# A loop over key places for the PV products of a decode-attention kernel, with fewer small products and one buffer for most of wo

## The chip, the cores and the metric

One core of a Trainium2 chip. The time is device microseconds (us) of one execution. The kernel before takes 357.53 us, the median of 3 runs (356.9 to 357.56).

Ratios are the mean time of one kernel's fast runs over that of the kernel before's fast runs of the same rounds, with a 95% interval, so they are not quite the quotient of the medians that are quoted beside them. The traces are of one profiled run each.

## The reference

One decode step of a transformer block with conditioned layer norms (cut to what matters; q has 32 heads, the caches 8 kv heads, so 4 q heads share a kv head; 32768 key places of 128 elements, all bfloat16):

```python
mod = silu(c) @ w_mod                       # six vectors: sa, ca, ga, sb, cb, gb
h = layernorm(x) * (1 + ca) + sa
q = (h @ wq)                                # 32 heads x 128
scores = q . k_cache * 128 ** -0.5          # per kv head: 4 x 32768
p = softmax(scores)
o = p @ v_cache                             # "PV"
x = x + ga * (o @ wo)
h = layernorm(x) * (1 + cb) + sb
x = x + gb * (relu(h @ w1) @ w2)
```

The K and V caches are 64 MiB each; with the weights the core reads 149 MB in one step.

## The kernel before

All big reads go through one DMA queue in a fixed order into a ring of four buffers. A buffer holds half of one kv head's K or V (4 MB); V of a head comes interleaved with K of the next head.

```python
ring = ctx.enter_context(tc.tile_pool(name="ring", bufs=4))
stream = [("wm",), ("wq",)] + [("k", 0, (2 * G, 2 * G + 1)) for G in range(NG)]
for g in range(LAST):
    for G in range(NG):
        stream += [(kind, gg, (2 * G, 2 * G + 1)) for kind, gg in (("k", g + 1), ("v", g))]
```

For each half of K, `scores` transposes it on VectorE in four pieces (`KTt`, three buffers) and multiplies on TensorE (`S_ps`, 32 products). `softmax` has three steps. The first takes the maximum (`m_p`, `mT_ps`, `Mrow`, `Mexp`). The second sends it back to all partitions (`Mb_ps` on TensorE, `nbias`), takes the exponential on ScalarE (`P_g`) and transposes it on VectorE (`PT_g`). The third is the sum and its reciprocal (`L_ps`, `Linv`). `pv` multiplies the transposed probabilities with V: 16 products for each 2 MB of V, so 32 for a buffer.

```python
def pe_order(instr):
    tc.stamp_issue_order_token(instr.ins, "pe_pv")    # keeps TensorE's order as written
# ... in pv:
    for j in js:
        m = nc.tensor.matmul(
            o_tiles[g][:], lhsT=PT_g[:, j, REP * s0:REP * (s0 + 4)],
            rhs=Vsb.rearrange("p (s j) d -> p s j d", j=16)[:, :, j, :],
            start=(u == 0 and j == 0), stop=(u == end and j == 15),
        )
        pe_order(m)
# ... in the main loop, for the second half of a head's V:
    stages = softmax(g + 1)
    pv(g, 2 * G, range(8))
    next(stages)                       # step 2 of the next head's softmax
    pv(g, 2 * G, range(8, 16))
    next(stages)
    pv(g, 2 * G + 1)
    next(stages, None)
```

So the author had put the steps of the next head's softmax between PV products, with order tokens that hold the scheduler to it.

## Time and profile before

| What | Number | Read from |
|---|---|---|
| span of the profiled run | 356.0 us | page, first line |
| queue of the big reads | 98.0% of the span | page, queues |
| a 4 MB tile, landing to landing | 9.67 us | landings in the trace |
| four tiles (a head) | 38.7 us | 4 x 9.67 |
| second PV of head 0 begins | 83.82 us | timeline |
| second PV of head 6 begins | 315.15 us | timeline |
| from there to the end of the span | 40.9 us | 356.0 - 315.15 |

The two starts give the **head period** used in this whole document: (315.15 - 83.82) / 6 = 38.56 us, the stream's pace. For every kernel below the span is cut the same way: start of the second PV of head 0, six heads, and the rest.

Two lines of the DMA queue's own waits (waited for: total us, times, longest) show what frees the buffers:

```profile
SPq L118 <- DVE KTt L375: 134.3, 15, 12.4
SPq L118 <- PE o_ps L458: 72.3, 8, 9.9
```

The queue waits for VectorE and TensorE to give buffers back, but the packets in flight keep the DMA engines busy all the while: the DMA row has a nine in 38 of its 40 slices, and the queue fills 98.0% of the span. So these waits cost nothing here.

### The profile page before, as it was taken

How to read it: one execution, taken by the hardware profiler on the slowest of the kernel's cores; microseconds unless marked ns; L12 is line 12 of the kernel's file. 1: busy time of each engine (PE TensorE's matmuls, PEld its weight loads, DVE VectorE, ACT ScalarE, POOL GpSimd, SP SyncE). 2: the span in 40 equal slices, each digit the busy share in tenths (PEclk: the TensorE clock that was granted, in tenths of full speed). 3: DMA queues.
4: the chain of work that ended last, by engine and by line, in shares of the span. 5: the costliest groups of instructions: out<-in, count | busy, mean ns of one | idle time of the engine just before them, and what ended most of it. 6: DMA issues, size and time to landing. Idle time of an engine off the chain costs nothing.

```text
span 356.0 us, 3635 instructions
## 1 busy us (share of the span) xinstructions
PE 287.1 (81%) x1571; PEld 128.5 (36%) x1571; DVE 191.6 (54%) x219; ACT 34.0 (10%) x78; POOL 8.5 (2%) x14
## 2 busy tenths in 40 slices
PE   0466965999699969788896969896978879799874
PEld 0253322444334433334332334333333424244473
DVE  8524697782667366463819373746637290842020
ACT  1023003102100110012000200012000200011020
POOL 9000000000000000000000000000000000000000
PEclk9966789999879998999899969999899969899755
DMA  8999999999999999999999999999999999999993
GB/s 326 437 435 436 423 443 427 422 446 427 429 438 435 420 447 431 423 442 429 431 438 427 433 439 423 438 436 423 435 442 419 442 431 422 442 427 419 390 407 138
DMA packets 6602, 149.66 MB, mean 420 GB/s; under 512 B 697, under 2 KB 698, under 8 KB 1594
## 3 DMA queue, kind: packets, MB, share of 16 engines
q1 hardware_dynamic: 6578, 149.43, 98.0%
q8 instruction: 12, 0.20, 0.2%
q14 instruction: 4, 0.03, 0.0%
q10 hardware_dynamic: 8, 0.00, 0.0%
HBM read 149.42 MB, written 0.00 MB: 420 GB/s over the span
## 4 chain that ended last, share of the span: by engine, by line
DMA 55%; PE 22%; DVE 16%; issue 4%; ACT 1%; SPq 0%; DVEq 0%; ACTq 0%
DMA Ksb<-in_A_k_cache_dram 50%; DVE KTt L375 14%; PE S_ps L384 9%; PE o_ps L458 6%; DMA c_row<-in_c_dram 3%; DMA w_sb<-in_B_w_dram 2%; PE modT_ps L284 1%; PE acc_ps L448 1%; PE q_ps L267 1%; PE mod_ps L267 1%; PE a_ps L510 1%; PE qT_ps L334 1%; PE acc_ps L468 1%; PE acc_ps L530 1%; ACT L243 0%
## 5 line engine op out<-in xcount | busy, mean ns | idle before, releaser
L384 PE MATMUL S_ps<-KTt,qbd 128*128 128x512 bf16 x512 | 135.6, 423 | 39.1 <-DVE KTt L375 39.1
L375 DVE STREAM_TRANSPOSE KTt<-Ksb 128x2048 f32<-128x2048 f32 x64 | 142.5, 2280 | 34.4 <-DMA Ksb<-in_A_k_cache_dram 32.8
L458 PE MATMUL o_ps<-Vsb,PT_g 128*16 128x512 bf16 x480 | 108.4, 379 | 0.0
L384 PEld LDWEIGHTS <-qbd 128*128 128x128 bf16 x512 | 53.4, 105 | 114.8 <-issue 64.4
L458 PEld LDWEIGHTS <-PT_g 128*16 128x16 bf16 x480 | 40.8, 90 | 60.0 <-issue 6.0
L390 DVE TENSOR_SCALAR_CACHE_REDUCE S_g<-S_ps 128x512 f32<-128x512 f32 x16 | 11.1, 692 | 37.7 <-PE S_ps L384 37.7
L355 ACT COPY qbd<-qrep_sb 32x128 bf16<-32x128 bf16 x32 | 9.4, 295 | 161.5 <-PE S_ps L384 160.4
L427 DVE STREAM_TRANSPOSE PT_g<-P_g 128x1024 bf16<-128x1024 bf16 x8 | 9.9, 1238 | 21.7 <-ACT P_g L422 21.7
L482 DVE TENSOR_TENSOR oT_sb<-acc_ps,Linv 128x4 bf16<-128x4 f32 x8 | 1.3, 162 | 25.7 <-PE acc_ps L448 17.2
L468 PE MATMUL acc_ps<-osel,X 16*128 16x4 f32 x64 | 8.4, 250 | 3.2 <-ACT X L466 3.2
L419 ACT ACTIVATE nbias<-Mb_ps 128x1 f32<-128x1 f32 x8 | 1.4, 171 | 89.1 <-PE Mb_ps L417 89.1
L203 PE MATMUL xc_ps<-one,c_bd 8*128 8x1 bf16 x4 | 0.3, 171 | 11.8 <-DVE c_bd L193 11.8
L468 PEld LDWEIGHTS acc_ps<-osel,X 16*128 16x128 f32 x64 | 7.7, 186 | 4.3 <-ACT X L466 4.3
L422 ACT ACTIVATE P_g<-S_g,nbias 128x1024 bf16<-128x1024 f32 x8 | 9.2, 1149 | 0.4 <-ACT nbias L419 0.2
L155 DVE COPY sel<-ident_bf 128x128 bf16<-128x128 bf16 x4 | 7.2, 3544 | 0.0
L466 ACT COPY X<-o_ps 16x512 f32<-16x512 f32 x8 | 4.6, 574 | 22.8 <-PE o_ps L458 22.8
L406 DVE TENSOR_REDUCE Mrow<-mT_ps 1x4 f32<-1x128 f32 x8 | 2.2, 278 | 8.2 <-PE mT_ps L404 8.2
L267 PE MATMUL q_ps<-wq_sb,hT 128*1 128x512 bf16 x32 | 3.6, 627 | 2.6 <-DVE hT L250 2.6
L435 DVE RECIPROCAL Linv<-L_ps 128x4 f32<-128x4 f32 x8 | 1.4, 176 | 7.0 <-PE L_ps L433 7.0
L417 PEld LDWEIGHTS Mb_ps<-ident_f,Mexp 1*128 1x128 f32 x16 | 2.3, 182 | 6.1 <-issue 6.1
L203 PEld LDWEIGHTS <-c_bd 8*128 8x128 bf16 x4 | 0.2, 112 | 11.8 <-DVE c_bd L193 11.8
L284 PE MATMUL modT_ps<-rowsel,mod_rows 128*128 128x4 f32 x16 | 3.9, 375 | 0.5 <-ACT mod_rows L279 0.5
(112 smaller groups left out, 96.6 us busy)
## 6 DMA issues: line engine op xcount, KB each, us to landing
Ksb<-in_A_k_cache_dram SPq DMA_DIRECT2D x16, 4096.0 KB, 29.7
Vsb<-in_A_v_cache_dram SPq DMA_DIRECT2D x15, 4096.0 KB, 28.9
wq_sb<-in_A_wq_dram SPq DMA_DIRECT2D x1, 4096.0 KB, 18.8
Vsb<-in_A_v_cache_dram SPq DMA_DIRECT2D x2, 2048.0 KB, 16.3
wm_sb<-in_w_mod_dram SPq DMA_DIRECT2D x1, 3072.0 KB, 10.3
wo_sb<-in_A_wo_dram SPq DMA_DIRECT2D x1, 2048.0 KB
wo_sb<-in_A_wo_dram SPq DMA_DIRECT2D x2, 1024.0 KB, 9.9
w_sb<-in_B_w_dram SPq DMA_DIRECT2D x1, 1792.0 KB, 9.9
```

Of the source, the lines that this page charges most:

```text
L155: nc.vector.tensor_copy(out=sel[:, hp, :].rearrange("p (a c) -> p a c", a=4), in_=src)
L267: nc.tensor.matmul(dst[j // 4][32 * (j % 4):32 * (j % 4) + 1, :], lhsT=src_T[:, kt:kt + 1], rhs=w[:, kt, j * 512:(j + 1) * 512], start=(kt ...
L284: nc.tensor.matmul(modT_ps[:, i, ko, :], lhsT=mod_rows[:, i, :].rearrange("q (m ko) -> q ko m", ko=KT)[:, ko, :], rhs=rowsel[:], start=Tru ...
L355: nc.scalar.copy(out=o, in_=i)
L375: nc.vector.transpose(out=KTt[:].bitcast(F32), in_=Ksb[:, 32 * half:32 * half + 32, :].rearrange("p j d -> p (j d)").bitcast(F32),)
L384: nc.tensor.matmul(S_ps, lhsT=qbd[g % 2][:, hp, s, :], rhs=KTv[:, 16 * sl:16 * sl + 16, h, :, par], start=(t4 == 0 and sl == 0 and hp == 0 ...
L390: nc.vector.tensor_scalar(out=S_tiles[g][:, G, :], in0=S_ps, scalar1=1.0, scalar2=None, op0=ALU.mult, op1=ALU.max, accum_out=m_tiles[g][:, ...
L422: nc.scalar.activation(out=P_g[:], in_=S_g[:].rearrange("p g f -> p (g f)"), func=ACT.Exp, bias=nbias[:], scale=scale, accum_out=l_g[:],)
L427: nc.vector.transpose(out=PT_g[:], in_=P_g[:])
L458: m = nc.tensor.matmul(o_tiles[g][:], lhsT=PT_g[:, j, REP * s0:REP * (s0 + 4)], rhs=Vsb.rearrange("p (s j) d -> p s j d", j=16)[:, :, j, : ...
L466: nc.scalar.copy(out=X[:], in_=o_tiles.pop(g)[:])
L468: nc.tensor.matmul(oT_ps, lhsT=X[:, s * Dh:(s + 1) * Dh], rhs=osel[:, s, :], start=(s == 0), stop=(g < LAST and s == 3), skip_group_check= ...
```

## The change

Its intent: write PV once as a loop that TensorE itself runs, to have fewer copies of instructions and less instruction fetch; replace many small TensorE products in the head and tail by a few larger ones; and put wo of the first six kv heads into one buffer of the ring, so that a slot is spared near the end. The core of the diff (cut):

```diff
-    WOP = [(0, Hkv // 2), (Hkv // 2, Hkv // 4), (3 * Hkv // 4, Hkv // 4)]
+    WOP = [(0, Hkv // 4), (Hkv // 4, Hkv // 2), (3 * Hkv // 4, Hkv // 4)]
...
-    stream += [("v", LAST, (0, 1)), ("v", LAST, (2,)), ("wo", 0), ("wo", 1), ("v", LAST, (3,)), ("wo", 2)]
+    stream += [("v", LAST, (0, 1)), ("v", LAST, (2,)), ("wo_mid", 0, 1), ("v", LAST, (3,)), ("wo", 2)]
...
-    def pe_order(instr):
-        tc.stamp_issue_order_token(instr.ins, "pe_pv")
...
+            nc.vector.memset(o_tiles[g][:], 0.0)
+        NJ = 4 // len(us)
+        PTv = PT_g.rearrange("p (a b) c -> p a b c", b=NJ)
+        with tc.tile_critical():
+            with nc.tensor.Fori(0, 16 // NJ) as turn:
+                for b in range(NJ):
+                    for u, V in zip(us, Vs):
+                        c0 = REP * 4 * (u % 2)
+                        nc.tensor.matmul(
+                            o_tiles[g][:], lhsT=PTv[:, bass.DynSlice(turn, 1), b, c0:c0 + 4 * REP],
+                            rhs=V.rearrange("p (s a b) d -> p s a b d", s=4, b=NJ)[:, :, bass.DynSlice(turn, 1), b, :],
+                            start=False, stop=False, skip_group_check=True,
+                        )
...
-            nc.scalar.copy(out=X[:], in_=o_tiles.pop(g)[:])
-            for s in range(4):
-                nc.tensor.matmul(oT_ps, lhsT=X[:, s * Dh:(s + 1) * Dh], rhs=osel[:, s, :], ...)
+        nc.vector.tensor_tensor(out=X[:], in0=o_tiles.pop(g)[:]..., in1=smask[:]..., op=ALU.mult)
+        nc.vector.tensor_reduce(out=Y[:], in_=X[:].rearrange("p s d -> p d s"), op=ALU.add, axis=AX.X)
+        nc.tensor.matmul(oT_ps, lhsT=Y[:], rhs=qsel, ...)
...
-                stages = softmax(g + 1)
-                pv(g, 2 * G, range(8))
-                next(stages)
-                pv(g, 2 * G, range(8, 16))
-                next(stages)
-                pv(g, 2 * G + 1)
-                next(stages, None)
+            if g < LAST or G == 0:
+                pv(g, (2 * G, 2 * G + 1))
                 continue
+        if g + 1 < Hkv:
+            stages = softmax(g + 1)
+            next(stages)
```

A loop makes 8 turns of 4 products for a 4 MB tile of V. It stands in a critical section, that is, in a block of its own. Since the loop is one piece, softmax's steps can no longer stand between its products, and the order tokens went with them.

## The prediction

> **What bounds the kernel now.** I read the page first (busy shares, the DMA row, the groups, the issues), then the wait list of the DMA queue, then the timeline of one head and of the tail. Page:

> ```profile
> span 356.0 us, 3635 instructions
> ...
> DMA  8999999999999999999999999999999999999993
> ...
> q1 hardware_dynamic: 6578, 149.43, 98.0%
> q8 instruction: 12, 0.20, 0.2%
> ...
> L384 PE MATMUL S_ps<-KTt,qbd 128*128 128x512 bf16 x512 | 135.6, 423 | 39.1 <-DVE KTt L375 39.1
> L375 DVE STREAM_TRANSPOSE KTt<-Ksb 128x2048 f32<-128x2048 f32 x64 | 142.5, 2280 | 34.4 <-DMA Ksb<-in_A_k_cache_dram 32.8
> L458 PE MATMUL o_ps<-Vsb,PT_g 128*16 128x512 bf16 x480 | 108.4, 379 | 0.0
> ...
> Ksb<-in_A_k_cache_dram SPq DMA_DIRECT2D x16, 4096.0 KB, 29.7
> Vsb<-in_A_v_cache_dram SPq DMA_DIRECT2D x15, 4096.0 KB, 28.9
> ```

> The stream is the bound: one queue fills 98.0% of the span. A 4 MB tile takes 29 us from issue to landing but tiles land about 9.67 us apart (landings at 283.25 and 292.92 us), so about three of the four slots are always in flight and compute has slack. A head is four tiles, 38.7 us. The timeline shows how that slack is made:

> ```profile
> 239.95 3.62 PE L458 MATMUL o_ps<-Vsb,PT_g 128*16 128x512 bf16 x16
> ...
> 240.26 1.15 ACT L422 ACTIVATE P_g<-S_g,nbias 128x1024 bf16<-128x1024 f32 x1
> ...
> 241.53 1.25 DVE L427 STREAM_TRANSPOSE PT_g<-P_g 128x1024 bf16<-128x1024 bf16 x1 [3.08 <-ACT P_g L422]
> ...
> 245.66 8.88 DVE L375 STREAM_TRANSPOSE KTt<-Ksb 128x2048 f32<-128x2048 f32 x4
> 248.02 8.78 PE L384 MATMUL S_ps<-KTt,qbd 128*128 128x512 bf16 x32 [2.73 <-DVE KTt L375]
> ...
> 256.72 7.07 PE L458 MATMUL o_ps<-Vsb,PT_g 128*16 128x512 bf16 x32
> ```

> The next head's softmax (exponential, transposition) runs on the other engines while TensorE does PV. Then one half-head is transpositions, 32 score products, 32 PV products. PV costs 7.07/32 = 0.221 us a product.

> The tail (the chain of waits, near its end):

> ```profile
> 331.74 0.58 ACT X L466
> ...
> 335.19 2.69 PE a_ps L510 x24
> ...
> 343.24 1.21 PE acc_ps L518 x32
> ...
> 344.46 7.63 DMA w_sb<-in_B_w_dram
> ```

> The last weight piece lands at 352.10, the span ends 3.9 us later; the tail on TensorE is only just ahead of the last bytes.

> [...] L448 issues 64 weight loads and products in 1.84 us, 29 ns a pair. [...] after the 2.73 us gap before 248.02 the 32 score products take 8.78 us, against 7.07 for 32 PV products. [...]

> **The change part by part.**

> Removed: copies of PV instructions (480 static products become 16 loops, 496 products), 64 small products of V tile 2 of the last head, three of every four products with osel, many small products in the head, some instruction fetch. Fetch is 0.2% of the DMA time; in the head and middle all this lies beside the stream. Value at most 1 us.

> Added, and decisive: each loop stands in a critical section, hence in its own block. The built program's TensorE list shows three things.
> a) Before every loop TensorE waits for the semaphores of *all* earlier work in program order, including the K tile issued after the V tile it needs. The loop of V(g,0) waits for K(g+1,1), one landing (9.67 us) later than before. About two tiles would still be in flight, so this alone does not drain the queue.
> b) Nothing crosses a block's edge. The softmax of head g+1 begins (max) before the second loop of head g, but its second step (Mb, exponential, transposition, sum) comes only after that loop. On VectorE it stands ahead of the next four K transpositions. So softmax and scores, once beside PV, follow it in series.
> c) Per product in the loop: one register instruction of several fused steps, then a product with two register addresses; per turn of four, an add and a compare-and-branch.

> Cost of a product, c[...] c = 0.272 us, above the 0.221 of the static product, so the sequencer sets the pace. A loop of 32: 8.7 us, plus about 0.6 for waits, drain and branches (my estimate): 9.3 us.

> After a first loop (half B): K has landed and three of four transpositions ran during the loop. 32 products 7.1, then the maxima 0.69+0.08+0.15, the transposition 0.3, Mrow 0.28, gaps 0.2: 8.8 us.

> After a second loop (half A): mask X about 0.7 (as the 0.69 of the scores' copy), Mexp 0.2, Mb and nbias about 0.55, exponential 1.15, transposition 1.25, Lexp 0.2, sum and reciprocal 0.7: 4.8. Then 11.1 from the first K transposition to the last score (245.66 to 256.80 in the timeline, half clock included), then the copy 0.8: 16.7 us.

> A head: 2 x 9.3 + 8.8 + 16.7 = 44.1 us against 38.7 of the stream. The bound moves from the DMA to this serial cycle of TensorE and VectorE.

> Path: the second loop of head 0 waits for K(2,0), which lands at 89.4 (99.08 - 9.67). Six heads on, 89.4 + 6 x 44.1 = 354.0, the second loop of head 6 begins. It ends at 363.3; softmax of head 7, now bare, 4.9: 368.2; its first loop 9.3: 377.5; the loop of V tile 2, 16 products: 5.0: 382.5; X, Y and a product 1.6; wo's rows 2.7; copy and join 2.7; 64 small products 1.8: 391.3. From there as before without its DMA wait: to w1's products 4.7, these 1.7, relu 0.2, w2's 1.8: 399.7. End of span 3.4 later: 403.1. Times stand about 1.5 above the span (357.53 against 356.0): **405 us**, 13% slower. Of the 47 us, some 33 come from six heads of 5.4 us; most of the rest from the tail, whose 7.1 us PV loops now wait for softmax and weights are asked for later.

> wo in one buffer: it frees a slot, so V tile 3 waits for the loop of V(6,1) rather than of V(7,0,1), one loop earlier; hidden behind the late TensorE chain. Worth 0 to 1 us.

> **The rivals.**
> R1, the stream stays the bound: c stays at or under 0.22. Then a head is 2 x 7.7 + 25.5 = 40.9 us, still over 38.7, and the path ends about 464 products x 0.051 = 24 us earlier: about 381. For it: the array itself can do 0.221. Against it: even then the series in (b) exceeds the stream.
> R2, all is hidden: the barrier's waits are met and softmax overlaps in some way I misread; the stream still ends near 350 and the time is 355 to 359. For it: DMA at 98% and 29 us of flight, deep slack. Against it: program order on TensorE puts Mb after the loop, and no slack in buffers cures a serial cycle longer than the stream's.
> R3, register addressing is dear, c = 0.35 to 0.40 us (fused steps taken one by one): 464 x 0.08 to 0.13 = 36 to 59 us more, 441 to 464.
> R4, the change gains: fewer fetches and no straggling last packet, 1 to 2 us, 355.5. The stream's own time cannot shrink: the bytes are the same.

> **Range and chances.** The time is nearly linear in c: 4.6 us per 10 ns. c from 0.21 to 0.36 gives 376 to 446; fixed terms are good to some 8 us, partly within that. Range 374 to 446. Slower by over 2% (above 364.7) needs only that (b) holds, 0.93; within 2%, R2, 0.06; faster by over 2% needs a stream below what 16 busy engines gave, 0.01.

> **What would show it.** Right: the DMA row falls from 9 to 7 or 8 in the middle; landing comes in less than 29 us after issue; TensorE's waits before the first K transposition of half A grow from 2.7 us to about 7; a head repeats every 44 us; loop products start 0.27 us apart. Step c is wrong if the spacing in a loop is 0.22 or 0.35; (b) is wrong if the exponential still overlaps PV products; (a) is wrong if loops begin before the following K tile lands. If heads still repeat every 38.7 us and only the tail grew, the middle was mis-sized and the time is under 372.

## The result, and the profile after

The changed kernel takes **420.62 us** (median of 4 runs, 418.56 to 422.01) beside 357.54 for the kernel before: ratio 1.176, 95% interval 1.170 to 1.183. Its results are correct. The page after, for the lines that were shown of before:

```profile
span 416.8 us, 4370 instructions
...
DMA  8999999999998995699888997899779959755282
...
q1 hardware_dynamic: 6592, 149.43, 85.8%
q8 instruction: 8, 0.13, 0.1%
...
L487 PE MATMUL o_ps<-Vsb,PT_g 128*16 x496 | 129.7, 395 | 32.6 <-issue 19.5
...
Ksb<-in_A_k_cache_dram SPq DMA_DIRECT2D x16, 4096.0 KB, 17.4
Vsb<-in_A_v_cache_dram SPq DMA_DIRECT2D x15, 4096.0 KB, 13.3
```

The same bytes in fewer fetches, but the queue fills 85.8% of the span and the DMA row has fives to eights from the middle on: the stream starves, because buffers come free late (the queue's waits for TensorE's sequencer at the loops, L482, come to 208.3 us in 16 waits). A tile lands 13 to 17 us after its issue in place of 29. There is no queue left to stand in, so the stream is no longer the bound.

The timeline of one head (columns: start, duration, engine, line, operation; in brackets the idle time before and what ended it; PEq is TensorE's sequencer), from its second loop to the next first loop (the view's window ends in that one, so only its first four products are counted):

```profile
229.00 8.71 PE L487 MATMUL o_ps<-Vsb,PT_g 128*16 x32 [1.23 <-DVE Mrow L429]
...
237.88 0.68 DVE L496 TENSOR_TENSOR X<-o_ps,smask 16x512 f32<-16x512 f32 x1 [9.79 <-PEq L482]
238.49 0.20 DVE L434 COPY Mexp<-Mrow 1x128 f32<-1x128 f32 x1
238.62 1.01 DVE L501 TENSOR_REDUCE Y<-X 16x128 f32<-16x512 f32 x1
238.75 0.22 PE L440 MATMUL Mb_ps<-ident_f,Mexp 1*128 1x1 f32 x1 [1.04 <-DVE Mexp L434]
...
239.21 1.15 ACT L445 ACTIVATE P_g<-S_g,nbias 128x1024 bf16<-128x1024 f32 x1
...
240.48 1.25 DVE L450 STREAM_TRANSPOSE PT_g<-P_g 128x1024 bf16<-128x1024 bf16 x1
...
242.68 8.86 DVE L401 STREAM_TRANSPOSE KTt<-Ksb 128x2048 f32<-128x2048 f32 x4
245.02 8.62 PE L410 MATMUL S_ps<-KTt,qbd 128*128 128x512 bf16 x32 [2.47 <-DVE KTt L401]
...
255.23 1.02 PE L487 MATMUL o_ps<-Vsb,PT_g 128*16 x4 [1.60 <-issue]
```

VectorE stands idle for 9.79 us while TensorE runs the loop. Then everything goes one after the other: X, Mexp, Mb, exponential, transposition of P, four transpositions of K, the scores. In the kernel before the exponential and the transposition of P lay beside PV products (shown in the prediction).

Where the span grew, by the three cuts:

| | before | after | more |
|---|---|---|---|
| second PV of head 0 begins | 83.82 | 90.51 | 6.7 |
| six heads | 231.3 (38.56 each) | 275.3 (45.88 each) | 43.9 |
| from the second PV of head 6 to the end | 40.9 | 51.0 | 10.2 |
| span | 356.0 | 416.8 | 60.8 |

### The profile page after: what moved, and what is told of

Its sections match the earlier page's. It is cut to its first block, busy times and chain, and to the rows that moved or that the text cites. A ratio compares the mean times of both kernels' runs of the same rounds, so it can differ in the third digit from the quotient of the medians.

```text
span 416.8 us, 4370 instructions
## 1 busy us (share of the span) xinstructions
PE 294.2 (71%) x1387; PEld 119.1 (29%) x1387; DVE 207.7 (50%) x251; ACT 29.0 (7%) x69; POOL 8.4 (2%) x14
## 3 DMA queue, kind: packets, MB, share of 16 engines
q1 hardware_dynamic: 6592, 149.43, 85.8%
## 5 line engine op out<-in xcount | busy, mean ns | idle before, releaser
L487 PE MATMUL o_ps<-Vsb,PT_g 128*16 x496 | 129.7, 395 | 32.6 <-issue 19.5
L410 PE MATMUL S_ps<-KTt,qbd 128*128 128x512 bf16 x512 | 129.1, 411 | 26.0 <-DVE KTt L401 22.0
L487 PEld LDWEIGHTS o_ps<-Vsb,PT_g 128*16 x496 | 44.2, 89 | 115.9 <-issue 84.9
L496 DVE TENSOR_TENSOR X<-o_ps,smask 16x512 f32<-16x512 f32 x8 | 5.4, 679 | 86.8 <-PEq L482 86.8
L416 DVE TENSOR_SCALAR_CACHE_REDUCE S_g<-S_ps 128x512 f32<-128x512 f32 x16 | 11.1, 692 | 40.8 <-PE S_ps L410 40.8
L456 PE MATMUL L_ps<-Lexp,ones_f 128*128 128x4 f32 x16 | 4.1, 326 | 15.6 <-DVE Lexp L453 15.6
L504 PE MATMUL acc_ps<-mask_sb,Y 16*128 16x4 f32 x16 | 3.2, 265 | 9.5 <-DVE Y L501 9.5
L456 PEld LDWEIGHTS L_ps<-Lexp,ones_f 128*128 128x128 f32 x16 | 3.8, 286 | 16.1 <-issue 16.0
L501 DVE TENSOR_REDUCE Y<-X 16x128 f32<-16x512 f32 x8 | 8.0, 1004 | 0.0
L427 PE MATMUL mT_ps<-ident_f,m_p 128*1 128x128 f32 x8 | 2.2, 270 | 8.3 <-DVE m_p L425 8.3
L504 PEld LDWEIGHTS acc_ps<-mask_sb,Y 16*128 16x128 f32 x16 | 2.5, 190 | 11.3 <-DVE Y L501 11.3
## 6 DMA issues: line engine op xcount, KB each, us to landing
Ksb<-in_A_k_cache_dram SPq DMA_DIRECT2D x16, 4096.0 KB, 17.4
Vsb<-in_A_v_cache_dram SPq DMA_DIRECT2D x15, 4096.0 KB, 13.3
wq_sb<-in_A_wq_dram SPq DMA_DIRECT2D x1, 4096.0 KB, 18.6
wo_sb<-in_A_wo_dram SPq DMA_DIRECT2D x1, 2048.0 KB, 10.7
```

Source lines behind the costliest of these rows:

```text
L410: nc.tensor.matmul(S_ps, lhsT=qbd[g % 2][:, hp, s, :], rhs=KTv[:, 16 * sl:16 * sl + 16, h, :, par], start=(t4 == 0 and sl == 0 and hp == 0 ...
L416: nc.vector.tensor_scalar(out=S_tiles[g][:, G, :], in0=S_ps, scalar1=1.0, scalar2=None, op0=ALU.mult, op1=ALU.max, accum_out=m_tiles[g][:, ...
L456: nc.tensor.matmul(L_ps[:], lhsT=ones_f[:], rhs=Lexp[:], start=True, stop=True)
L487: nc.tensor.matmul(o_tiles[g][:], lhsT=PTv[:, bass.DynSlice(turn, 1), b, c0:c0 + 4 * REP], rhs=V.rearrange("p (s a b) d -> p s a b d", s=4 ...
L496: nc.vector.tensor_tensor(out=X[:], in0=o_tiles.pop(g)[:].rearrange("p (s d) -> p s d", s=4), in1=smask[:].unsqueeze(2).to_broadcast([16, ...
L501: nc.vector.tensor_reduce(out=Y[:], in_=X[:].rearrange("p s d -> p d s"), op=ALU.add, axis=AX.X)
```

## The experiments

The theory at the outset was this. A head is a serial cycle of two loops, half A (from the end of a head's second loop to the next loop) and half B (from the end of a first loop to the second). In the changed kernel it exceeds the stream's 38.7 us. Three parts of the change could make it long: the loop's pace per product, the critical section with its waits, and softmax's second step behind the second loop (the order). The rivals were that one of the three alone makes the loss. The first four runs take the parts away one by one; "order" in the tables means where softmax's second step stands.

### e1: the turns written out inside the critical section

```diff
-            with nc.tensor.Fori(0, 16 // NJ) as turn:
-                for b in range(NJ): ...
+            for j in range(16):
+                for u, V in zip(us, Vs): ...      # static addresses, still in tile_critical
```

> Changed kernel with each loop's turns written out as static products, still inside the critical section (same blocks, same waits before, same order). Theory T (loop pace and serial order both cost): a product falls from 0.2725 to about 0.22 us, 464 of them are worth 464 x 0.053 = 24 us: about 396 us, head period near 42.5 us, still above the stream's 38.7. Rival A (the loop's pace is all of the loss): 357 to 362 us. Rival B (the pace lies beside something else): 415 us or more.

Measured: 396.63 us (ratio 1.108, 1.102 to 1.114), head period 42.90. The loop's pace is worth 24.0 us, as the theory had it. 39 us of the loss are left, so rival A is out.

### e2: eight products a turn

```diff
-        NJ = 4 // len(us)
+        NJ = 8 // len(us)
```

> Loop kept, 8 products a turn in place of 4, so half the turn ends. Theory T (the cost is one stalled turn end, about 0.23 us with its taken branch; the register step per product hides behind the array): the mean product falls from 0.2725 to about 0.245 or, if a turn end overlaps more, 0.22: 395 to 408 us. Rival, the composition written in the prediction [...]: mean product 0.252 us, 464 x 0.020 = 9 us less: about 411 us. The spacing inside a turn tells them apart whatever the total: 0.215 us under T[...].

Measured: 408.69 us (ratio 1.141, 1.136 to 1.147), just outside the theory's range and near the rival's 411. The total would mislead here. The windows of one first and one second loop (columns: window; its length; busy us and count of PE, PEld (TensorE's weight loads), DVE, ACT, POOL; granted clock, the share of TensorE's full speed that it ran at; DMA share; GB/s) tell what happened. The changed kernel:

```profile
210.40:219.20 8.80, 8.18 (x32) 2.71 (x32) 5.75 (x3) 0.00 (x0) 0.00 (x0) 1.00 0.78 335
229.00:237.70 8.70, 8.19 (x32) 2.72 (x32) 0.00 (x0) 0.00 (x0) 0.00 (x0) 1.00 0.98 422
```

Eight products a turn:

```profile
207.40:214.50 7.10, 7.08 (x32) 2.79 (x32) 5.76 (x3) 0.00 (x0) 0.00 (x0) 1.00 0.88 378
224.30:233.10 8.80, 8.74 (x32) 3.25 (x32) 0.00 (x0) 0.00 (x0) 0.00 (x0) 0.81 0.97 421
```

The first loop falls to 7.08 us, the time of 32 static products (7.07 in the kernel before). All its starts are 215 or 216 ns apart, with one of 234; the rival, which put more of the cost on each product and less on a turn's end, is refuted. In the second loop the granted clock is 0.81: eight products there are 410 to 427 ns apart, at half clock (in the changed kernel's trace, where the granted clock is 0.50 from 92.0 to 94.2 us, products start 426 or 427 ns apart), and the loop is as long as before. TensorE had idled 2.6 us ahead of it, but for one small product. In the changed kernel much the same idle time stands there (2.4 to 2.8 us in heads 1 to 6), and five of its seven second loops ran at full clock. In the other two (heads 0 and 5) the half-clock stretch let the sequencer get ahead: after it the products are 215 to 223 ns apart to the loop's end, at the turns' ends too, and the loops were hardly longer, 8.8 and 9.1 us. So e2 gained in one loop of two: seven second loops at 1.7 us each are about 12 us of the 24 us that e1 gained.

### e3 and e4: no loop and no critical section; then the order of before as well

```diff
 # e3: in pv
-        with tc.tile_critical():
-            with nc.tensor.Fori(0, 16 // NJ) as turn: ...
+        for j in range(16):
+            for u, V in zip(us, Vs): ...          # static addresses
 # e4: e3, and the tokens "pe_pv" and the staging of the kernel before
+                stages = softmax(g + 1)
+                pv(g, (2 * G, 2 * G + 1), range(4))
+                next(stages)
+                pv(g, (2 * G, 2 * G + 1), range(4, 8))
+                next(stages)
+                pv(g, (2 * G, 2 * G + 1), range(8, 16))
+                next(stages, None)
```

> Changed kernel with static products and no critical section, but the changed order: softmax's second step stands behind the second PV of a head on TensorE. Theory T: blocks and barriers gone as well as the loop's pace; half A stays serial at about 15.5 us, a head about 37 us, just under the stream's 38.7: 357 to 365 us. Rival C (order alone makes the head longer than the stream): 375 to 390 us, head period 40 or more.

> Changed kernel with static products, no critical section, and the order of the kernel before given back (softmax's steps between PV products). What is left of the change: masked reduction in place of four osel products, smaller head and tail, wo of six kv heads in one buffer. Theory T: the stream is the bound again, 355 to 358 us, head period 38.7. Rival: the small parts cost by themselves, 362 us or more.

Measured: e3 360.30 us (ratio 1.007, 1.005 to 1.009), head period 39.01; e4 357.11 us (ratio 0.998, 0.997 to 1.000), head period 38.57. All of the loss is in the loop, its block and the order; what remains of the change in e4 (fewer small products, wo in one buffer) gains about 0.4 us (0.1 to 1.3 by the interval). The engines' shares of the chain that ended last, first e3:

```profile
PE 70%; DVE 18%; DMA 8%; issue 2%; ACT 1%; SPq 0%; DVEq 0%
```

and e4:

```profile
DMA 74%; DVE 16%; issue 5%; PE 4%; SPq 0%; DVEq 0%
```

With the order behind PV the chain runs through TensorE and VectorE at 39.0 us a head, with the order of before through the stream. In time they are 3 us apart, because 39.0 is so near to the stream's 38.7.

### e5 and e6: from the kernel before, the order alone and the weight split alone

```diff
 # e5: from the kernel before
-        tc.stamp_issue_order_token(instr.ins, "pe_pv")
+        pass
 ...   # and softmax requested after the second PV, as in the changed kernel
 # e6: from the kernel before
-    WOP = [(0, Hkv // 2), (Hkv // 2, Hkv // 4), (3 * Hkv // 4, Hkv // 4)]
+    WOP = [(0, Hkv // 4), (Hkv // 4, Hkv // 2), (3 * Hkv // 4, Hkv // 4)]
 ...   # and "wo_mid": both parts loaded into one buffer
```

> Kernel before with one thing changed: the order tokens and the staging of softmax between PV products are dropped, so softmax's second step comes behind the second PV, as in the changed kernel; no loop, no critical section. Theory T after e3 and e4 (order alone costs about 3 us because it brings TensorE's own cycle to about 39 us a head, level with the stream's 38.7): 359 to 362 us. Rival, the prediction's reading that this series is what lengthens the head: 375 us or more.

> Kernel before with only the weight split changed: wo of the first six kv heads in one buffer of the ring, of the last two in another. All theories: hidden behind the stream, 356.5 to 358 us; a gain or loss of over 1 us would mean that the last tiles' buffers set the end.

Measured: e5 363.12 us (ratio 1.014, 1.012 to 1.017), head period 38.95: the cycle as expected, the total 1 us over the range. The order alone costs 5.4 us, not the 63 of the change. e6 357.17 us (ratio 0.998, 0.996 to 1.001): nothing that can be told from zero.

### e7 and e8: K transpositions ahead of P's on VectorE, with 4 and 8 products a turn

```diff
+            tc.stamp_issue_order_token(kt.ins, "dve_kp")       # each K transposition
...
+        tc.stamp_issue_order_token(pt.ins, "dve_kp")           # PT, Lexp, Linv behind them
...
-                if stages is not None:
-                    next(stages, None)
+            if stages is not None:                             # after both halves' scores
+                next(stages, None)
+                next(stages, None)
 # e8 as well
-        NJ = 4 // len(us)
+        NJ = 8 // len(us)
```

> Changed kernel with its loop, but on VectorE the four transpositions of the next K tile stand ahead of the transposition of P and of the sum's reciprocal, and TensorE has the next scores ahead of the sum. Theory T (half A is a serial chain in which softmax's second step delays the K transpositions): scores start 2 to 4.5 us sooner after a second loop, head period 41.5 to 44 in place of 45.9, 393 to 408 us. Rival (the chain is led by something else, such as the arrival of K or the entry of the loop, and P's transposition simply comes as late): 416 us or more.

> The order of the run before (K transpositions ahead of P's) and 8 products a turn together. If both gains are on the same chain they add: from 408.7 us with 8 a turn, less 12 to 27 us: 382 to 397 us. The rival of the run before: 405 us or more. Second loops should still meet a half-clock stretch where TensorE idles about 2.5 us ahead of them.

Measured: e7 411.63 us (ratio 1.149, 1.145 to 1.153): outside both ranges. The head period did fall as expected, to 43.75 us, which is 12.8 us over six heads, but the token also held back head 0, whose second loop began at 97.50 in place of 90.51. e8 390.41 us (ratio 1.093, 1.089 to 1.097), period 41.01, in its range. Half A is a chain in which VectorE's order counts; but X still stood ahead of the K transpositions and waited for the loop.

### e9 and e10: softmax and K transpositions beside the second loop

The step that the others had not tried: leave loop and critical section as they are and put the work around them in another order.

```diff
+        tc.stamp_issue_order_token(mb.ins, "pe_pv")            # Mb ...
+                        tc.stamp_issue_order_token(m.ins, "pe_pv")   # ... ahead of the loop's products
+        tc.stamp_issue_order_token(pt.ins, "dve_kp")           # VectorE: PT, then K transpositions, then X
+            tc.stamp_issue_order_token(kt.ins, "dve_kp")
+        tc.stamp_issue_order_token(x.ins, "dve_kp")
...
+            if G == 0 and deferred:                            # X, Y, normalise after the next scores
+                settle(deferred.pop())
+            if g < LAST and G == NG - 1:                       # two steps ahead of the second loop
+                stages = softmax(g + 1)
+                next(stages)
+                next(stages)
```

> Changed kernel with its loop of 4 products a turn and its critical sections, but with another order around them: softmax's Mb goes ahead of the second loop on TensorE, so the exponential, P's transposition and three of the next four K transpositions run beside that loop; the masked reduction of the finished head (X, Y) comes after those transpositions. Theory T (the loss is the serial cycle of TensorE and VectorE, made longer by the loop but not by the loop alone): a head is two loops of 8.7, half A near 10.3 and half B near 10.5, 38.2 us, at the stream's 38.7: 357 to 368 us, the DMA row back at 9s. Rival (a loop in a critical section costs what it costs wherever softmax stands; the waits before its blocks bind): head 41 us or more, 375 us or more.

> The same with 8 products a turn. Theory T: TensorE's cycle falls to about 35 to 37 us, well under the stream's; 355 to 361 us, equal to the kernel before within 1 per cent. Rival as for the run before: 370 us or more.

Measured: e9 394.11 us (ratio 1.101, 1.097 to 1.106), period 41.19; e10 375.98 us (ratio 1.052, 1.048 to 1.056), period 38.38. Both totals fell on the rival's side, so the theory was in doubt until the trace was read. In e9, after a second loop that ended at 186.42:

```profile
187.16 0.18 DVE L461 RECIPROCAL Linv<-L_ps 128x4 f32<-128x4 f32 x1 [7.81 <-PE L_ps L459]
187.25 8.86 DVE L401 STREAM_TRANSPOSE KTt<-Ksb 128x2048 f32<-128x2048 f32 x4
189.59 1.89 PE L411 MATMUL S_ps<-KTt,qbd 128*128 128x512 bf16 x8 [2.47 <-DVE KTt L401]
```

VectorE idled 7.81 us for `Linv`, which waits for a TensorE product that stands behind the loop; the K transpositions queued behind it. In the heads where `Linv` stood elsewhere the scores began 0.2 us after the loop. Head 0's second loop was also late (96.73). Both are faults of the experiment, not of the loop.

### e11 and e12: the same, mended

```diff
+            if g > 1 and u < 2:                                # tokens only where they serve
+                tc.stamp_issue_order_token(kt.ins, "dve_kp")
...
+        if g > 0:
+            tc.stamp_issue_order_token(li.ins, "dve_kp")       # Linv behind the K transpositions
```

> The free order (e9) mended in two places that its trace showed: the reciprocal of the sum no longer stands ahead of the K transpositions on VectorE in half of the heads (it waited there for a product behind the loop, 3.2 us before the scores in place of 0.2), and the order is not forced on head 0, where it held the second loop back by 6 us. 4 products a turn. Theory T: head 38 to 39 us, second loop of head 0 near 90.5, six heads on 319 to 325, then about 49 us to the end as in e9: 369 to 376 us. Rival (the blocks and their waits hold a head at 41 us whatever the order): 386 us or more.

> The same with 8 products a turn. Theory T: TensorE's own cycle about 36 us, so the stream paces the heads at 38.7 or a little less while TensorE catches up; second loop of head 0 near 90.5, second loop of head 6 at 315 to 322, 47 us to the end as in e10: 363 to 371 us. What then remains over the kernel before is the late second loop of head 0 and the tail. Rival: heads at 38.4 with no catching up and the tail as late as in e10, 372 us or more.

Measured: e11 **372.86 us** (ratio 1.043, 1.040 to 1.046), period 38.80; e12 371.27 us (ratio 1.040, 1.036 to 1.045), period 38.76, a little over its range. The DMA row of e11 and one second loop with what lies beside it:

```profile
DMA  8999999999999999999999999999999999994482
```

```profile
283.26 0.22 PE L442 MATMUL Mb_ps<-ident_f,Mexp 1*128 1x1 f32 x1 [0.62 <-DVE Mexp L436]
...
284.80 8.88 PE L494 MATMUL o_ps<-Vsb,PT_g 128*16 x32 [1.32 <-issue]
285.00 1.25 DVE L453 STREAM_TRANSPOSE PT_g<-P_g 128x1024 bf16<-128x1024 bf16 x1 [1.79 <-ACT P_g L448]
...
286.26 6.69 DVE L401 STREAM_TRANSPOSE KTt<-Ksb 128x2048 f32<-128x2048 f32 x3
...
293.87 7.09 PE L412 MATMUL S_ps<-KTt,qbd 128*128 128x512 bf16 x32 [0.19 <-PEq L489]
```

P's transposition and three K transpositions run inside the loop's 8.88 us, the scores follow it after 0.19 us at full clock, and the row has its nines back until the last buffers. The same loop, of the same 4 products a turn and in the same critical section, now costs 15 us and not 63. Its pace no longer counts either: going to 8 a turn is worth 1.6 us here and was worth 12 in e2. (As in e2, the second loops gained little: all seven in e12 ran partly at half clock, 8.6 to 9.9 us each.)

What holds e12 from going lower is the wait before each loop. The built program of the changed kernel shows TensorE's instruction at the head of a loop's block (the names are semaphores of the DMA rings and the engines):

```
L672 UnconditionalBranch [waits DMAHW2_49,DMAHW1_49,DMAHW3_49,DMAHW0_49,DMAHW4_49,PE_sequencer_49,
                          DMAHW5_49,DVE_49,DMAHW6_49,PE_49,DMAHW7_49,Activation_49,Pool_49]
```

The trace shows these thirteen waits as six instructions of two each and a branch with the last, at L672 of the changed kernel and at L698 of e11. In e11 the K tiles that come after the V tile in the stream landed at 205.73, 225.15, 283.18 and 302.60, and loops began at 206.88, 226.21, 284.80 and 303.66: 1.1 to 1.6 us after each (the trace's semaphore records have the others too: all 14 loops of heads 0 to 6 begin 1.0 to 1.6 us after the landing of the tile behind theirs in the stream). In e12 the scores ahead of the loop at 206.48 ended 1.8 us sooner than in e11 and the loop began only 0.4 us sooner; the time between grew from 3.42 to 4.79 us. The K tile had landed at the same time in both (205.73 and 205.66). These loops are paced by the landing of a tile that they do not use. The second loop of head 6 begins at 323.13 in e11 and at 313.50 in e4: 9.63 us, one landing. The rest of e11's span after that start is 47.9 us, in e4 42.0. The two differences, 9.6 and 5.9, are the 15.5 us between the spans of e11 and e4.

### All runs in one table

| run | PV | order | us | head period |
|---|---|---|---|---|
| before | static | between PV products | 357.5 | 38.56 |
| changed | loop, 4 a turn | behind the second loop | 420.6 | 45.88 |
| e1 | static, critical section | behind | 396.6 | 42.90 |
| e2 | loop, 8 a turn | behind | 408.7 | 44.68 |
| e3 | static | behind | 360.3 | 39.01 |
| e4 | static | between PV products | 357.1 | 38.57 |
| e5 | before's static | behind | 363.1 | 38.95 |
| e6 | before, weight split alone | between PV products | 357.2 | 37.77 |
| e7 | loop, 4 | behind, K first | 411.6 | 43.75 |
| e8 | loop, 8 | behind, K first | 390.4 | 41.01 |
| e9 | loop, 4 | beside the loop, with faults | 394.1 | 41.19 |
| e10 | loop, 8 | beside the loop, with faults | 376.0 | 38.38 |
| e11 | loop, 4 | beside the loop | 372.9 | 38.80 |
| e12 | loop, 8 | beside the loop | 371.3 | 38.76 |

A period under the stream's 38.7 belongs to a kernel that catches up: in e6 and e10 the second PV of head 0 began late (86.83 and 96.78) and the six heads after it made up for a part of that.

Taken away in one sequence (changed, e1, e3, e4) the pace is worth 24 us, the critical section 36, the order 3. In another (changed, e11, e12, e4) the order is worth 48, the pace 2, and what separates e12 from e4 (the critical section with the loop in it, and a somewhat different order) 14. Neither list is wrong: costs on one serial cycle beside a stream do not add. The cycle is two PV stretches and halves A and B, the stream is 38.7 us, and a head takes the longer of the two. In e3 the serial cycle, at 39.0, has just reached the stream; all that is put on it from there (e1: waits and series at the blocks' ends, 3.9 us a head; then the loop's pace, 3.0 us a head) is paid in full. In e11 the same pace is put on a cycle with room.

No version beats the kernel before by more than the 0.2% of e4, which counts as the same.

## Why the prediction was right or wrong

The prediction, 405 us and slower by over 2% with a chance of 0.93, was right in direction and in the bound, and 15.6 us too low, inside its range.

**The bound moves to a serial cycle of TensorE and VectorE.** Right. Head period 45.88 for the 44.1 of the text, the DMA row broken, landings 13 to 17 us after issue. The scores began 7.2 to 9.3 us after a second loop, for the "about 7" of the text.

**Where the 15.6 us are.** The second loop of head 0 began at 90.51 (89.4 predicted): 1.1. Six heads: 6 x (45.88 - 44.1) = 10.7. From the second loop of head 6 to the end: 51.0 against 403.1 - 354.0 = 49.1: 1.9. The median stands 3.8 us above the profiled span and not 1.5: 2.3. (The sum is 0.4 more than 15.6 because the text rounded 404.6 up to 405.) So the head was the mis-sized term. Of it, the loops were right: 8.7 us each. With the 0.6 of waits that the text put with each loop, its author's estimate, half B was to be 9.4 and was 9.7 to 10.0; half A was to be 17.3 and was 18.6 in the mean of six (18.49, 20.46, 17.87, 17.52, 17.40, 19.60). A term left out of half A is the end of a wo part: in the two heads that end one (20.46 and 19.60), the product of `spread` stands ahead of Mb on TensorE, and Mb begins 2.97 us after the loop in place of 1.04. These two heads have 5.5 of the 7.5 us by which half A exceeds the text's over six heads; the other four stood at 17.4 to 18.5. Y, 1.01 us, which the text had not listed, added little: it ran beside Mb and the exponential, and P's transposition began 0.12 us after the exponential (240.36 and 240.48 in the timeline above).

**Step c, 0.272 us a product.** This was the estimate: no loop runs in the kernel before, so its trace could not show it. The total was right (8.7 us for 32 products), its parts were wrong. The text put more on each product and less on the end of a turn than the trace shows. Measured, the sequencer takes about 155 ns a product (the next register step starts 29 ns, the median, after a weight load), which hides behind the array's 215, and about 0.47 us more at a turn's end, of which 0.23 show. Two errors of opposite sign gave 0.272. It mattered: by the text's parts 8 a turn would run at 0.252 us, and it ran at 0.216.

**Step (a), the wait for all earlier work.** Right as a mechanism. In the changed kernel it counts only at the start, since the later tiles have landed by then: without the section (e3) the second loop of head 0 begins 7.4 us sooner. "This alone does not drain the queue" is borne out by e11 and e12. What the text did not say is that the wait remains as one landing, 9.6 us, at the end of a stream that is the bound again.

**Step (b), nothing crosses a block's edge.** This is the step that failed as the text put it. The series was there and was decisive, but the edge does not impose it: in e11 the blocks stand and VectorE works through P's transposition and three K transpositions beside the loop. What imposed it was the order on the engines: Mb behind the loop, and X, which waits for the loop, ahead of everything on VectorE. That order came with the dropped tokens and staging, for e3, with no block at all, has its softmax behind PV too. And series alone was not enough: e3 and e5 have it at 39 us a head. It took the series, the blocks' waits and the loop's pace together to pass the stream by 7 us a head.

**The rivals.** R1 (c at or under 0.22 gives 381) was tried by e1: c was about 0.221 in most loops and the time 396.6, for the head fell to 42.9 and not 40.9; halves A and B were the under-sized terms again. R2 (all is hidden) was false for the change as written; with another order, e11, the heads come near it (38.80 us) but the total does not (372.9 for its 355 to 359). R3 (c of 0.35 to 0.40) was false: c was 0.272. R4 (fewer fetches and a better end gain 1 to 2 us) is in e4: 0.4 us.

**Left open.** Why TensorE's clock halves in some second loops and not in others after much the same idle time was not tried by itself. Of heads 1 to 6 it halved in all six in e2, after gaps of 2.5 to 2.7 us with one small product in each, in three in e8, and in one in the changed kernel, after 2.76 us; the other five there, at full clock, had gaps of 2.43 to 2.58 us. Nor was the tail of e11, 5.9 us longer than e4's, taken apart.

## What to carry to other kernels

The largest cost of the loop here was the freedom to put other work between its products. Before writing one, list which work stood there, and order it so that other engines run it beside the loop: here that alone was worth 48 of 63 us. Once that was done, the loop's pace mattered little (1.6 us), while the wait at its entry still cost one landing, 9.6 us. Give a turn enough products for the sequencer's lead to cover the turn's end (here a lead of some 60 ns a product against 0.47 us, so that eight hid it and four did not), and look whether the loop's entry waits for transfers that the loop does not read.

When parts of a change lie on one serial cycle beside a stream, do not add up their single costs: compare the cycle's length with the stream's, and read spacings in the trace as well as totals, for e2's total agreed with the wrong composition.
